# Another order for the first batch item of a fused attention and maxout-MLP kernel

One core of one Trainium2 chip. The metric is the device time of one launch in microseconds (us), the median of the runs. All other times are us from the start of the profiled span, unless marked ns.

## The reference, cut

```python
# q, k, v: [4, 8, 768, 64] fp32; sort_net: [4, 8, 8, 8]
for _ in range(5):                      # softmax rows, then normalise columns
    P = softmax_rows(P); P = P / P.sum(-2)
k_sorted = einsum('bhij,bhjcd->bhicd', P, k_blocks)     # 8 blocks of 96 rows
v_sorted = einsum('bhij,bhjcd->bhicd', P, v_blocks)
x = softmax(q_b @ k_sb.T / 8) @ v_sb    # inside each block, then heads side by side: [3072, 512]
out = maximum(x @ w1, x @ w2) @ w_out   # w1, w2: [512, 1024], w_out: [1024, 512]
```

The kernel uses max(a, b) = relu(a - b) + b: it forms W1 - W2 on VectorE (`w_difference`), h = x(W1 - W2), g = relu(h), and folds W2·W_out into one matrix, for which W2 is transposed (`w2_transposes`).

## The kernel before

These are the parts that the argument needs. The kernel gives TensorE, ScalarE (ACT) and VectorE (DVE) their instructions in program order, and in the timelines ACT and DVE run them in that order. "A" and "D" name the engine that evicts a PSUM tile.

```python
psum = tile_pool(bufs=4)                # four PSUM tiles in all
def keep_streaming(ps, n): ...          # filler: n columns of matmuls on zeros into a fresh tile

load_v(0, 0, 3); load_k(0); load_q(0)   # one queue, in this order
load_w(w2_sb, moe_w2)
load_w_columns(w1_sb, moe_w1, 0, 1); load_w_columns(w1_sb, moe_w1, 1, 2); load_w_columns(w1_sb, moe_w1, 2, 4)
...
def turn_v(rows, eng, c0, c1):          # v's (c, d) turned to (d, c)
    dst = v_dc[rows, 0 : D * BLK].rearrange("p (d c) -> p d c", c=BLK)[:, :, c0:c1]
    src = v_raw[rows].rearrange("p (c d) -> p d c", d=D)[:, :, c0:c1]
    ...                                 # nc.scalar.copy or nc.vector.tensor_copy
...
def moe_h_products(b, ch, t, hps, n=0):
    if hps[0] == 0:
        h_ps[0] = ps_f32("h_ps"); keep_streaming(h_ps[0], n)
    for m in range(2):
        for hp in hps: matmul(h_ps[0][:, m*512 : m*512+TCH], ..., start=(hp == 0), stop=(hp == 3))
...
# the first batch item
sort_k(0, 0, 3072, "A"); sort_k(0, 1, 256, "A"); sort_k(0, 2, 256, "D")
q_transposes(0, 0, "A"); sort_v(0, 0, 256, "D"); q_transposes(0, 1, "A"); sort_v(0, 1, 256, "D")
scores(0, 0, 512); sort_v(0, 2, 256, "D"); SC[1](); sort_v(0, 3, 256, "A")
...                                     # selections
SC[2](); SC[3](); VA[0](); VA[1](); values(0, 2, 1024); VA[3]()
w_difference(0); SC[4](); x_transposes(0, 0, "A"); w2_out = w2_transposes(0, "D")
x_transposes(0, 1, "A"); w_difference(1); moe_h(0, 0, 0, "A", n=1024); w2_out(); SC[5]()
# then: VA4, w_difference(2); h tile 1, SC6, SC7, VA5, w_difference(3); h tile 2, ...
```

`SC[u]` are scores u with their exp (e) on ACT, `VA[u]` values u with their normalisation on DVE.

The softmax here doesn't subtract the row's maximum and nothing guards it: scores larger than these inputs give would overflow.

## Time and profile before

| | before |
|---|---|
| median (range) of the first 3 runs | 186.23 (185.96 to 186.98) |
| span of the profiled run | 184.2 |
| granted clock over the span | 1.000 |
| first query transpose, start | 15.80 |
| g of h tile 0, start | 29.37 |
| third h product, start | 32.17 |
| fourth h product, start | 34.53 |

The last four rows are read from the timeline of TensorE and ACT. From the fourth h product on, both kernels run the same order. In rows of the timeline and of the chain of work, the first number is the start and the second the length. Groups of matmuls are named by the PSUM tile they write: tq query transposes, v_ps v sorts, s_ps scores, o_ps values, tx x transposes, tw W2 transposes, h_ps h products.

### The profile page before, as it was taken

What the parts mean: (1) busy time and instruction counts of PE and PEld (TensorE: products, weight loads), DVE (VectorE), ACT (ScalarE), POOL (GpSimd) and SP (SyncE); (2) the same over time, 40 slices, a digit from 0 to 9 for tenths busy, and PEclk for the clock granted to TensorE, in tenths of its full rate; (3) what the DMA queues carried; (4) which work ended last, traced back from release to release, by engine and by line L of the source; (5) the groups of instructions that cost most, each with busy time, mean ns of one, the idle gap of its engine ahead of it and who ended that gap; (6) DMA issues with size and microseconds to landing.
All of it is one profiled execution on the core that took longest, in us unless ns stands there. A gap on an engine that the chain in (4) does not pass through costs nothing.

```text
span 184.2 us, 4604 instructions
## 1 busy us (share of the span) xinstructions
PE 172.1 (93%) x2050; PEld 102.7 (56%) x2069; DVE 95.5 (52%) x189; ACT 93.8 (51%) x111; POOL 21.5 (12%) x38
## 2 busy tenths in 40 slices
PE   7969789999999899999999999999999999999990
PEld 2337675756564555557655555767645456654460
DVE  5887796669722655284816544355526444420030
ACT  3599866779447504355956451665463513431001
POOL 7851222200450000002000000000000000000000
PEclk9999999999999999999999999999999999999999
DMA  3999999999199972036600220200002032000241
GB/s 60 202 202 211 201 206 216 191 204 190 21 175 219 202 202 104 12 117 75 99 0 4 114 105 12 114 4 4 0 5 114 0 117 114 0 0 4 114 166 61
DMA packets 13427, 19.17 MB, mean 104 GB/s; under 512 B 800, under 2 KB 7840, under 8 KB 13408
## 3 DMA queue, kind: packets, MB, share of 16 engines
q0 software_dynamic: 9792, 12.58, 40.3%
q1 hardware_dynamic: 3328, 6.10, 8.6%
q8 instruction: 16, 0.26, 0.6%
q10 hardware_dynamic: 288, 0.20, 0.3%
q14 instruction: 3, 0.02, 0.0%
HBM read 25.17 MB, written 6.29 MB: 171 GB/s over the span
## 4 chain that ended last, share of the span: by engine, by line
PE 80%; DMA 7%; ACT 4%; DVE 3%; issue 2%; POOL 2%; ACTq 0%; POOLq 0%
PE out_ps L557 32%; PE h_ps L530 22%; DMA q_raw<-in_q_dram 6%; PE v_ps L370 4%; PE wc_ps L498 4%; PE o_ps L420 4%; PE k_ps L349 3%; PE s_ps L395 3%; PE tx_ps L452 3%; PE tq_ps L319 2%; DVE o L98 1%; ACT o L96 1%; DMA out_dram<-o 1%; PE tw_ps L475 1%; PE tq_ps L324 1%
## 5 line engine op out<-in xcount | busy, mean ns | idle before, releaser
L557 PE MATMUL out_ps<-wo_sb,g 128*128 128x512 bf16 (+1 forms) x185 | 46.0, 370 | 2.4 <-ACT o L96 0.7
L530 PE MATMUL h_ps<-xT,w_sb 128*128 128x384 bf16 x256 | 46.4, 326 | 0.3
L544 ACT ACTIVATE g<-h_ps 128x768 bf16<-128x768 f32 x27 | 21.9, 812 | 21.0 <-PE h_ps L530 21.0
L403 ACT ACTIVATE e<-s_ps 96x768 bf16<-96x768 f32 x32 | 24.3, 803 | 15.9 <-PE s_ps L395 15.9
L530 PEld LDWEIGHTS <-w_sb 128*128 128x128 bf16 x256 | 23.5, 98 | 14.9 <-issue 0.5
L557 PEld LDWEIGHTS <-g 128*128 128x128 bf16 x200 | 17.4, 98 | 16.6 <-issue 1.3
L557 PE MATMUL out_ps<-wc,xT 128*128 128x512 bf16 (+1 forms) x100 | 24.8, 370 | 0.0
L437 DVE TENSOR_TENSOR x<-o_ps,rs 96x512 bf16<-96x512 f32 x32 | 22.0, 686 | 1.1
L431 DVE RECIPROCAL rs<-o_ps 96x8 f32<-96x8 f32 x32 | 6.4, 200 | 25.5 <-PE o_ps L420 25.4
L98 DVE CAST v_sb<-v_ps 96x1024 bf16<-96x1024 f32 x9 | 11.0, 1221 | 12.2 <-PE v_ps L370 12.2
L96 ACT COPY o<-out_ps 128x1024 f32<-128x1024 f32 x6 | 6.1, 1012 | 19.6 <-PE out_ps L557 10.0
L557 PEld LDWEIGHTS <-xT 128*128 128x128 bf16 x100 | 9.8, 98 | 11.0
L98 DVE COPY o<-out_ps 128x1024 f32<-128x1024 f32 x5 | 6.1, 1225 | 16.3 <-PE out_ps L557 16.3
L188 DVE COPY v_dc<-v_raw 64x1536 bf16<-64x1536 bf16 (+2 forms) x9 | 14.0, 1591 | 0.0
L420 PEld LDWEIGHTS <-e 96*128 96x128 bf16 x256 | 11.2, 98 | 4.8 <-issue 0.6
L420 PE MATMUL o_ps<-v_sb,e 96*128 96x65 bf16 x256 | 12.7, 194 | 0.7 <-ACT v_sb L96 0.6
L370 PEld LDWEIGHTS <-v_dc 64*128 64x128 bf16 x256 | 8.1, 95 | 3.4 <-issue 2.4
L96 ACT CAST kT<-k_ps 128x1024 bf16<-128x1024 f32 x10 | 9.9, 1010 | 0.0
L78 PE MATMUL pe<-fill 128*128 128x512 bf16 x26 | 8.7, 512 | 1.2 <-DVE fill L72 1.2
L96 ACT COPY xT<-tx_ps 128x768 bf16<-128x768 bf16 x9 | 7.2, 795 | 5.1 <-PE tx_ps L452 5.1
L96 ACT CAST v_sb<-v_ps 96x1024 bf16<-96x1024 f32 x7 | 7.0, 1015 | 5.4 <-PE v_ps L370 5.4
L370 PE MATMUL v_ps<-bd,v_dc 64*128 64x64 bf16 x256 | 9.5, 190 | 0.0
(74 smaller groups left out, 164.0 us busy)
## 6 DMA issues: line engine op xcount, KB each, us to landing
out_dram<-o SPq DMA_DIRECT2D x11, 512.0 KB, 2.8
k_raw<-in_k_dram POOLq DMA_DIRECT2D x12, 256.0 KB, 13.7
q_raw<-in_q_dram POOLq DMA_DIRECT2D x4, 768.0 KB, 9.4
v_raw<-in_v_dram POOLq DMA_DIRECT2D x6, 384.0 KB, 11.9
w_sb<-in_moe_w_dram POOLq DMA_DIRECT2D x3, 512.0 KB, 15.1
wo_sb<-in_moe_w_out_dram POOLq DMA_DIRECT2D x2, 512.0 KB, 19.8
v_raw<-in_v_dram POOLq DMA_DIRECT2D x3, 256.0 KB, 5.0
w_sb<-in_moe_w_dram POOLq DMA_DIRECT2D x2, 256.0 KB, 15.7
```

The source lines that it names most:

```text
L78: nc.tensor.matmul(ps[:, 0:w], fill[:, 0:128], fill[:, 0:w], start=True, stop=True)
L96: nc.scalar.copy(out=out_ap, in_=in_ap)
L98: nc.vector.tensor_copy(out=out_ap, in_=in_ap)
L188: nc.vector.tensor_copy(out=dst, in_=src)
L370: nc.tensor.matmul(ps[:, m * 64 : (m + 1) * 64], v_dc[r0 : r0 + 64, d * BLK : d * BLK + 128], bd_v[b][r0 : r0 + 64, :], start=True, stop=True,
L403: nc.scalar.activation(out=e[:, 0 : 8 * BLK].rearrange("p (t f) -> p t f", t=2), in_=ps[0:BLK].rearrange("p (t f) -> p t f", t=2)[:, :, 0 ...
L420: nc.tensor.matmul(ps[:, h2 * 512 + ii * 65 : h2 * 512 + (ii + 1) * 65], e[:, (h2 * 4 + ii) * BLK : (h2 * 4 + ii) * BLK + 128], v_sb[:, m0 ...
L437: nc.vector.tensor_tensor(out=x, in0=ov[:, :, :, 0:D], in1=rs.to_broadcast([BLK, 2, 4, D]), op=ALU.mult,)
L498: nc.tensor.matmul(wc_ps[0][:, m * 512 : (m + 1) * 512], w2T[:, fb, dmt * 128 : (dmt + 1) * 128], wo_sb[:, fb, :], start=(fb == 0), stop=( ...
L530: nc.tensor.matmul(h_ps[0][:, m * 512 : m * 512 + TCH], w1_sb[:, hp, fb * 128 : (fb + 1) * 128], xT[:, b % 2, ch, hp % 2, hp // 2, :], sta ...
L544: nc.scalar.activation(out=g, in_=src, func=AF.Relu)
L557: nc.tensor.matmul(dst, g_tiles[b, ch, m // 2][:, m % 2, off : off + 128] if m < NFB else xT[:, b % 2, ch, hp % 2, hp // 2, off : off + 12 ...
```

## The change

Its intent: sort all of v before the second query half, so that values can follow the first scores at once; have the keys' block diagonal sooner; begin the h products of two tiles when only half of xT is there; and have the first columns of W1 and W2 early enough for that. The diff, cut:

```diff
-    load_w(w2_sb, moe_w2)
+    load_w_columns(w2_sb, moe_w2, 0, 2)
     load_w_columns(w1_sb, moe_w1, 0, 1)
     load_w_columns(w1_sb, moe_w1, 1, 2)
+    load_w_columns(w2_sb, moe_w2, 2, 4)
     load_w_columns(w1_sb, moe_w1, 2, 4)
@@ turn_v: a new argument flip; with it the copy's loops are (c, d), d innermost
+            dst = v_dc[rows, 0 : D * BLK].rearrange("p (d c) -> p c d", c=BLK)[:, c0:c1]
+            src = v_raw[rows].rearrange("p (c d) -> p c d", d=D)[:, c0:c1]
@@ block_diagonals: keys' product, reduction and result first, then those of the values
@@ moe_h_products: h_ps[t] in place of h_ps[0]
@@ the softmax steps
-            turn_v(first, "A", 0, 8)    ...  turn_v(first, "A", 8, 16)
-    turn_v(first, "A", 16, 32)
+            turn_v(first, "A", 0, 11)   ...  turn_v(first, "A", 11, 22)
+    turn_v(first, "A", 22, 32, True)
@@ the first batch item, as it is afterwards
+    sort_k(0, 0, 3072, "A"); sort_k(0, 1, 512, "A"); sort_k(0, 2, 256, "D")
+    q_transposes(0, 0, "D")
+    sort_v(0, 0, 0, "A"); sort_v(0, 1, 256, "D"); sort_v(0, 2, 256, "A"); sort_v(0, 3, 256, "D")
+    scores(0, 0, 256); SC[1]()
+    q_transposes(0, 1, "A")
+    w_difference(0)
+    values(0, 0, 1024); VA[1](); SC[2](); SC[3](); values(0, 2, 512); VA[3]()
+    x_transposes(0, 0, "A"); SC[4]()
+    moe_h_products(0, 0, 0, (0, 2), 512)
+    x_transposes(0, 1, "A"); w_difference(1)
+    moe_h_products(0, 0, 1, (0, 2))
+    moe_h(0, 0, 0, "A", (1, 3))
+    ...                                  # selections
+    SC[5](); w2_transposes(0, "D")()
@@ later: h tile 1 is finished where it was computed
+            units[1] = lambda: moe_h(0, 0, 1, "A", (1, 3))
```

More of the change, by code (lines that the diff above doesn't have):

```diff
@@ L179, with turn_v @@
     load_k(1)
-    def turn_v(rows, eng, c0, c1):
-        dst = v_dc[rows, 0 : D * BLK].rearrange("p (d c) -> p d c", c=BLK)[:, :, c0:c1]
-        src = v_raw[rows].rearrange("p (c d) -> p d c", d=D)[:, :, c0:c1]
+    def turn_v(rows, eng, c0, c1, flip=False):
+        if flip:
+            dst = v_dc[rows, 0 : D * BLK].rearrange("p (d c) -> p c d", c=BLK)[:, c0:c1]
+            src = v_raw[rows].rearrange("p (c d) -> p c d", d=D)[:, c0:c1]
+        else:
+            dst = v_dc[rows, 0 : D * BLK].rearrange("p (d c) -> p d c", c=BLK)[:, :, c0:c1]
+            src = v_raw[rows].rearrange("p (c d) -> p d c", d=D)[:, :, c0:c1]
         if eng == "A":
@@ L255, in block_diagonals @@
         keep_streaming(pe, n)
-        kinds = [1] if b % 2 else [0, 1]
+        kinds = [1] if b % 2 else [1, 0]
         for m in kinds:
@@ L269, in block_diagonals @@
             )
-        m0, nk = kinds[0], len(kinds)
-        pm = const.tile([128, 2, NB, NB], FP32, tag="pm", name="pm")
         for m in kinds:
+            pm = const.tile([128, NB, NB], FP32, tag=f"pm{m}", name="pm")
             nc.vector.tensor_tensor(
-                out=pm[:, m],
+                out=pm,
                 in0=pe[:, m * 64 : m * 64 + 64].rearrange("p (i j) -> p i j", j=NB),
@@ L278, in block_diagonals @@
             )
-        pt = const.tile([128, 2, NB], FP32, tag="pt", name="pt")
-        nc.vector.reduce_sum(out=pt[:, m0:2], in_=pm[:, m0:2], axis=AX.X)
-        bd = const.tile([128, 2, 8, NB], BF16, tag=f"bd{b}", name="bd")
-        for m in kinds:
+            pt = const.tile([128, NB], FP32, tag=f"pt{m}", name="pt")
+            nc.vector.reduce_sum(out=pt, in_=pm, axis=AX.X)
+            bd = const.tile([128, 8, NB], BF16, tag=f"bd{m}{b}", name="bd")
             nc.vector.tensor_tensor(
-                out=bd[:, m],
+                out=bd,
                 in0=maskM[:, m].to_broadcast([128, 8, NB]),
-                in1=pt[:, m].to_broadcast([128, NB, 8]).transpose([0, 2, 1]),
+                in1=pt.to_broadcast([128, NB, 8]).transpose([0, 2, 1]),
                 op=ALU.mult,
             )
-        if b % 2 == 0:
-            bd_v[b] = bd_v[b + 1] = bd[:, 0].rearrange("p m i -> p (m i)")
-        bd_k[b] = bd[:, 1].rearrange("p m i -> p (m i)")
+            if m:
+                bd_k[b] = bd.rearrange("p m i -> p (m i)")
+            else:
+                bd_v[b] = bd_v[b + 1] = bd.rearrange("p m i -> p (m i)")
     v_sb = big.tile([BLK, 128, D + 2], BF16, tag="v_sb", name="v_sb")
@@ L524, in moe_h_products @@
         if hps[0] == 0:
-            h_ps[0] = ps_f32("h_ps")
-            keep_streaming(h_ps[0], n)
+            h_ps[t] = ps_f32("h_ps")
+            keep_streaming(h_ps[t], n)
         for m in range(2):
@@ L530, in moe_h_products @@
                 nc.tensor.matmul(
-                    h_ps[0][:, m * 512 : m * 512 + TCH],
+                    h_ps[t][:, m * 512 : m * 512 + TCH],
                     w1_sb[:, hp, fb * 128 : (fb + 1) * 128],
@@ L539, in moe_h @@
         moe_h_products(b, ch, t, hps, n)
-        ps = h_ps[0]
+        ps = h_ps[t]
         g = gpool.tile([128, 2, TCH], BF16, tag="g", name="g")
@@ L616 @@
             selections(0)
-            turn_v(first, "A", 0, 8)
+            turn_v(first, "A", 0, 11)
         if it == 3:
-            turn_v(first, "A", 8, 16)
-    turn_v(first, "A", 16, 32)
+            turn_v(first, "A", 11, 22)
+    turn_v(first, "A", 22, 32, True)
     turn_v(first, "A", 32, 40)
@@ L627 @@
     sort_k(0, 0, 3072, "A")
-    sort_k(0, 1, 256, "A")
+    sort_k(0, 1, 512, "A")
     sort_k(0, 2, 256, "D")
-    q_transposes(0, 0, "A")
-    sort_v(0, 0, 256, "D")
-    q_transposes(0, 1, "A")
-    sort_v(0, 1, 256, "D")
-    scores(0, 0, 512)
-    sort_v(0, 2, 256, "D")
-    SC[1]()
-    sort_v(0, 3, 256, "A")
+    q_transposes(0, 0, "D")
+    sort_v(0, 0, 0, "A")
+    sort_v(0, 1, 256, "D")
+    sort_v(0, 2, 256, "A")
+    sort_v(0, 3, 256, "D")
+    scores(0, 0, 256)
+    SC[1]()
+    q_transposes(0, 1, "A")
+    w_difference(0)
+    values(0, 0, 1024)
+    VA[1]()
+    SC[2]()
+    SC[3]()
+    values(0, 2, 512)
+    VA[3]()
+    x_transposes(0, 0, "A")
+    SC[4]()
+    moe_h_products(0, 0, 0, (0, 2), 512)
+    x_transposes(0, 1, "A")
+    w_difference(1)
+    moe_h_products(0, 0, 1, (0, 2))
+    moe_h(0, 0, 0, "A", (1, 3))
     for b in range(1, B):
         selections(b)
-    SC[2]()
-    SC[3]()
-    VA[0]()
-    VA[1]()
-    values(0, 2, 1024)
-    VA[3]()
-    w_difference(0)
-    SC[4]()
-    x_transposes(0, 0, "A")
-    w2_out = w2_transposes(0, "D")
-    x_transposes(0, 1, "A")
-    w_difference(1)
-    moe_h(0, 0, 0, "A", n=1024)
-    w2_out()
     SC[5]()
+    w2_transposes(0, "D")()
     def turn(rows, c0):
```

## The prediction

> **What bounds the kernel now.** I read the busy slices first, then the stretches of the span, then the chain of work that ended last, then the timeline of the first 40 us for TensorE, ScalarE (ACT) and VectorE (DVE). Times are us from the span's start.
>
> The stretches (busy time of each engine in each):
>
> ```profile
> 0.00:15.80 15.80, 12.60 (x133) 5.74 (x133) 12.04 (x58) 10.38 (x13) 10.04 (x20) 1.00 0.94 162
> 15.80:37.20 21.40, 19.64 (x344) 14.41 (x346) 15.32 (x29) 16.15 (x20) 5.20 (x9) 1.00 1.20 205
> 37.20:75.00 37.80, 36.86 (x442) 21.24 (x448) 21.89 (x36) 19.28 (x22) 4.62 (x8) 1.00 0.83 160
> ```
>
> The first number after the comma is TensorE. From 37 us on it is busy 97% (36.86 of 37.80), the granted clock is 1.00 throughout, and the change touches nothing there but the list of who evicts what. So the change can act only before 37 us, and what it wins or loses there should be handed on to the end almost in full.
>
> The chain in that part (start, length, what):
>
> ```profile
> 5.07 10.68 DMA q_raw<-in_q_dram
> ...
> 15.80 0.86 PE tq_ps L324 x24
> ...
> 21.02 0.81 ACT e L403
> 21.82 0.99 ACT v_sb L96
> ...
> 22.86 0.67 PE o_ps L420 x16
> ...
> 27.35 0.81 ACT xT L96
> ...
> 28.20 1.14 PE h_ps L530 x6
> 29.33 0.28 PE s_ps L395 x8
> 29.61 0.36 PE o_ps L420 x8
> 29.97 1.32 PE h_ps L530 x8
> 31.31 0.82 ACT g L544
> ...
> 32.17 1.47 PE h_ps L530 x8
> 33.67 0.82 ACT g L544
> ...
> 34.53 1.46 PE h_ps L530 x8
> ```
>
> Two things are to be seen. Until 15.76 the end is set by the load of q, issued at 5.07; nothing ahead of it in the queue changes. After that, TensorE and the evictions take turns: e, v_sb, xT and g on ACT are links of the chain.
>
> The four PSUM tiles go round: tile n is given out when tile n-4 has been evicted. Counting the allocations from the code, the third h tile is 29 and the second is 25, and the timeline agrees: that eviction (g) ends at 31.31 + 0.81 = 32.12 and the third h product starts at 32.17. So there is some 0.05 from an eviction's end to the matmul behind it. I use this rule for the new order.
>
> **What the Trainium skill says.** (1) "PSUM — Partial Sum Buffer", the four PSUM rules: an output lies in one 2 KiB bank, and a group's first matmul clears the bits of its whole bank. The two halves of an h tile are 512 columns each, so a bank each, and a product begun on half of xT may stay open while other tiles are written. No profile of before shows this; it has no half-begun product. (2) "ScalarE: Activation LUTs", What ACT_TABLE_LOAD costs: 186 ns + 0.833 ns per element, and ACTIVATEs behind each other overlap by about 93 ns. The trace agrees for e (768 elements: 826 ns by the page, 803 measured; a pair takes 1.50, so 0.70 from start to start). It disagrees for the turning copies of v: 512 elements should be 613 ns and take 1050 to 1066, 1024 take 2046, so 1.9 ns an element or 0.12 us a column. (3) "DMA: Bandwidth & Descriptors", Issuing engines are not separate DMA queues: all transfers share 16 engines, so moving W pieces only changes their order; the trace moves about 205 GB/s all through the start. (4) "TensorE: Matmul & The Clock Gate", What's actually happening: the clock drops after an idle window of some 3.4 us. The clock stays 1.00 before, and no gap that I find below is over 1.1 us, so I charge nothing for the changed filler matmuls.
>
> **The change part by part.**
>
> *Keys' block diagonal first, turning of v.* Before, the two masks' products, one reduction and the two results run from 11.69 to 12.76 on DVE, then the first key sort starts at 12.98. With the keys' three operations alone (0.23, 0.22, 0.22, some 0.73 with gaps, as for the second item at 37.40) they are ready at 12.42, and the filler ends at 12.87: about 0.1 sooner. One more reduction makes DVE's turning copy end at about 15.4, not 15.11. ACT turns 22 columns in its idle time among the softmax steps, not 16: 6 x 0.12 = 0.7 sooner free, so its key casts start at 13.9, not 14.55. All of it lies beside the q load, which ends at 15.76. Worth 0.
>
> *W by columns.* The queue's waits let me date the landings: first half of W2 near 19.6, second 21.8, first W1 columns 23.1. Issued by columns, the first W1 columns come 0.26 MB, or 1.3 us at 205 GB/s, after the first W2 piece: about 20.9. Before, the first W difference runs at 26.66, long after its data. So this only makes the earlier place in DVE's order possible. Worth 0 itself.
>
> *New order from 15.80.* Durations: query transposes 0.79 of TensorE per half, a v sort 0.56, filler of 256 0.21, scores 0.25, values 0.27, x transposes 0.35, W2 transposes 0.87, a whole h product 1.30 and so a half 0.65; ACT v_sb 1.01, qT 1.44, e 0.81, xT 0.79, g 0.81 (0.09 less from start to start); DVE v_sb 1.22, qT 0.95, values' pair 0.83.
> - TensorE: first query half to 16.59, four v sorts with three fillers to 19.46 (16.59 + 4 x 0.56 + 3 x 0.21), filler and scores 0 and 1 to 20.20, second query half to 21.00, filler and values 0 and 1 to 21.97. Values 0 start at 21.45, against 22.86 before: a lead of 1.4.
> - ACT: v_sb to 18.28 and to 19.81, e0 20.05 to 20.86, e1 to 21.57, then qT's second half to 22.91 (1.44 behind e1). Scores 2 need it: TensorE waits from 21.97 to 22.96. This takes 1.0 of the lead.
> - Scores 2 and 3 to 23.46; e2 to 24.16, e3 to 24.87; values 2 at 24.22, values 3 at 24.92 to 25.20. Two waits on ACT, 0.8 together with the filler in them.
> - x transposes 0 to 25.56, xT 25.72 to 26.51; scores 4; half of h0 from 26.56 to 27.20; x transposes 1 to 27.55; xT 27.72 to 28.51; meanwhile half of h1; rest of h0 28.56 to 29.20; its g starts at 29.37. Before, that g starts at 29.37 too. The 1.4 are spent.
> - What is done by then: before, h0 and the first W2 transposes (0.87); after, h0 and half of h1 (0.65). After is 0.2 behind.
> - Now the PSUM tiles. After: scores 5 to 29.45; the W2 transposes take h0's tile, so they wait for g0 (30.18) until 30.24 and run to 31.10: 0.8 of waiting. Values 4 and the rest of h1 to 32.02, its g to 33.00. Scores 6 take h1's tile, so they start at 33.05: 1.0 of waiting, with nothing put beside it. Scores 6, 7 and values 5 to 33.80, third h at 33.98 (its W difference is behind the later W2 copy on DVE). Before it is at 32.17. There, scores 6, 7 and values 5 ran while g was being made, so that the round trip was filled.
> - Balance at the third h product: 33.98 - 32.17 = +1.8. Sum: 0.2 behind, + 0.8 + 1.0 waits, + 0.2 for the W difference, - 0.4 of waiting that before has at this place (31.8 to 32.17).
>
> From there both have the same order and both wait for g before the fourth h. So 186.23 + 1.8 = 188.0 by the plain sum.
>
> *Side effect.* The host-side balance of ACT against DVE starts from other totals (I worked through it: 12 of 82 later evictions change engine, among them o of the second and third item and a g). TensorE idles only 2.1 in all between 37 us and the end for evictions and the like, so I put it at plus or minus 0.5.
>
> **The rivals.**
> (A) *The lead holds.* Values start 1.4 sooner and the h products start sooner; if ACT delivers qT's second half sooner than 22.9, or h0 ends by 27.5, the end comes 1 us sooner: about 185.2. For it: the change has been laid out with care (filler sizes, exactly four tiles between the h1 halves), which smells of tuning against the chip. Against: e1 and qT on ACT in program order.
> (B) *Nothing moves*, as the load of q and then W, v and k paces the start anyway: 186.2. For it: about 205 GB/s until 45 us. Against: after 15.8 the chain of before holds no load.
> (C) *ACT's and PSUM's round trips replace the waits removed*: +1.8, 188.0, as above.
> (D) *W late*: if the first W1 columns land at 23 and not 20.9, the W difference at the head of DVE holds up the values' evictions and everything after: another +0.5 to 1, 188.8.
>
> **Range and chances.** C is what the arithmetic gives, but it sums twenty steps of which several may be off by 0.2, and A has the care of the layout for it. I weigh C and D together at 70%, B at 12% and A at 18%, and take a little off C: 187.6. Range 185.2 to 189.2. Faster by over 2% means below 182.5, which is more than all the waits before 37 us hold: 2%. Slower by over 2% means above 189.95, for which D must add itself to C: 4%. Within 2%: 94%.
>
> **What would show it.** Right: query transposes still start at 15.80; values 0 near 21.5; a wait of some 1.0 before scores 2 released by ACT's qT; g0 near 29.4; a wait of 0.8 before the W2 transposes and of 1.0 before scores 6, both released by ACT's g; the third h product near 34.0. Wrong: g0 before 28.5, or TensorE busy through 29 to 33 us; a W difference waiting for a load (then D); another start of the query transposes; or a stretch after 37 us whose length differs by over 0.5, which would be the changed evictions.

## The result, and the profile after

The changed kernel took 188.52 us (median of 4 runs, 187.97 to 188.58), the kernel before 186.09 (185.95 to 186.98). The ratio is 1.0114, with a 95% interval of 1.0076 to 1.0151. Here and below a ratio is the mean time of one kernel's fast runs over that of the other's in the same rounds, so not quite the ratio of the medians. The verdict is: slower by 1.1%, which is within 2%.

The busy slices of the changed kernel have a line that the kernel before does not have (its line holds nines alone):

```profile
PEclk9999699999999999999999999999999999999999
```

The stretches of the changed kernel (TensorE, weight loads, DVE, ACT, GpSimd, then granted clock, DMA share and GB/s), to be laid beside those in the prediction:

```profile
15.80:37.20 21.40, 18.96 (x313) 13.40 (x314) 14.20 (x27) 15.05 (x19) 5.18 (x9) 0.92 1.22 205
37.20:75.00 37.80, 37.19 (x460) 21.85 (x459) 22.26 (x38) 20.41 (x24) 4.62 (x8) 1.00 0.79 147
```

In the first stretch the mean clock is 0.92 and TensorE issues 313 matmuls where it issued 344. After 37 us nothing got worse. In finer stretches (TensorE alone) the changed kernel shows where the clock went:

```profile
18.00:20.00 2.00, 1.92 (x47) 1.00 1.43 192
20.00:22.00 2.00, 1.97 (x34) 0.54 1.28 206
22.00:24.00 2.00, 2.00 (x31) 0.60 1.26 213
24.00:26.00 2.00, 1.54 (x32) 1.00 1.22 200
```

For 3.4 us from 20.2 on, TensorE ran at half clock. The chain of work through the changed part:

```profile
15.68 1.82 ACT kT L96 x2
17.50 0.04 issue
17.54 0.27 PE v_ps L78
...
20.54 0.76 PE s_ps L399 x16
21.30 1.44 PE tq_ps L328 x23
...
22.76 1.45 ACT qT L96
...
24.25 0.36 PE s_ps L399 x8
...
30.70 0.28 PE s_ps L399 x8
30.97 1.01 PE tw_ps L479 x16
...
32.01 1.22 DVE w2T L98
...
33.41 0.57 issue
33.99 0.69 DVE w_sb L514
...
34.72 1.49 PE h_ps L534 x8
```

Three things differ from the prediction. The second v sort waits for ACT's key casts, which end at 17.50. The second query transposes take 1.44 at half clock, not 0.79. And the third h product waits for a W difference on DVE. What the prediction had right is the wait of scores 2 (24.25) for ACT's qT, right behind it.

The W2 transposes start at 30.97, while this eviction of h tile 0 (timeline of the changed kernel) is still running, until 31.54:

```profile
30.73 0.81 ACT L548 ACTIVATE g<-h_ps 128x768 bf16<-128x768 f32 x1 [0.90 <-PE h_ps L534]
```

So they did not wait for that tile. Scores 6 did not wait for h tile 1 either: they start in the timeline before its eviction (32.92 to 33.73) does.

```profile
32.81 0.82 PE L399 MATMUL s_ps<-qT,kT 64*128 64x96 bf16 x16
```

| from the timelines | before | after | difference |
|---|---|---|---|
| first query transpose to start of g0 ("head") | 13.57 | 14.91 | +1.34 |
| start of g0 to third h product ("tail") | 2.80 | 3.99 | +1.19 |
| third to fourth h product | 2.36 | 2.37 | 0.01 |
| fourth h product to end of span | 149.7 | 149.7 | 0 |

The spans differ by 2.6 (186.8 against 184.2), and all of it arises between 15.8 and 34.7. The twelve later evictions that change engine cost nothing that shows.

### The profile page after: what moved, and what is told of

It is laid out like the page before. It is cut to its first block, busy times and chain, and to the rows that moved or that the text cites. A ratio compares the mean times of both kernels' runs of the same rounds, so it can differ in the third digit from the quotient of the medians.

```text
span 186.8 us, 4622 instructions
## 1 busy us (share of the span) xinstructions
PE 175.1 (94%) x2068; PEld 103.6 (55%) x2068; DVE 95.7 (51%) x191; ACT 95.1 (51%) x111; POOL 22.9 (12%) x38
## 4 chain that ended last, share of the span: by engine, by line
PE 79%; ACT 8%; DVE 8%; DMA 2%; issue 1%; ACTq 0%
PE out_ps L561 32%; PE h_ps L534 22%; PE v_ps L374 4%; PE wc_ps L502 4%; ACT v_dc L191 3%; PE o_ps L424 3%; PE s_ps L399 3%; PE k_ps L353 3%; PE tx_ps L456 3%; PE tq_ps L323 2%; DVE o L98 1%; DMA out_dram<-o 1%; PE tw_ps L479 1%; ACT kT L96 1%; ACT e L407 1%
## 5 line engine op out<-in xcount | busy, mean ns | idle before, releaser
L561 PE MATMUL out_ps<-wo_sb,g 128*128 128x512 bf16 (+1 forms) x200 | 48.1, 371 | 1.4 <-DVE o L98 0.6
L548 ACT ACTIVATE g<-h_ps 128x768 bf16<-128x768 f32 x26 | 21.1, 812 | 21.4 <-PE h_ps L534 21.4
L98 DVE COPY o<-out_ps 128x1024 f32<-128x1024 f32 x6 | 7.3, 1224 | 17.8 <-PE out_ps L561 17.8
L98 DVE CAST v_sb<-v_ps 96x1024 bf16<-96x1024 f32 x7 | 8.5, 1220 | 12.0 <-PE v_ps L374 12.0
L96 ACT COPY o<-out_ps 128x1024 f32<-128x1024 f32 x5 | 5.1, 1012 | 17.6 <-PE out_ps L561 17.6
L550 DVE TENSOR_SCALAR g<-h_ps 128x768 bf16<-128x768 f32 x6 | 5.7, 957 | 12.3 <-PE h_ps L534 12.3
L96 ACT CAST v_sb<-v_ps 96x1024 bf16<-96x1024 f32 x9 | 8.9, 1014 | 5.8 <-PE v_ps L374 5.8
L122 POOL DMA_DIRECT2D q_raw<-in_q_dram x4 | 5.7, 1433 | 46.9 <-DVE q_pair L308 44.5
L96 ACT COPY xT<-tx_ps 128x768 bf16<-128x768 bf16 x10 | 8.0, 796 | 5.2 <-PE tx_ps L456 5.2
## 6 DMA issues: line engine op xcount, KB each, us to landing
w_sb<-in_moe_w_dram POOLq DMA_DIRECT2D x3, 512.0 KB, 15.8
```

The lines of the kernel that those rows point to most:

```text
L96: nc.scalar.copy(out=out_ap, in_=in_ap)
L98: nc.vector.tensor_copy(out=out_ap, in_=in_ap)
L548: nc.scalar.activation(out=g, in_=src, func=AF.Relu)
L561: nc.tensor.matmul(dst, g_tiles[b, ch, m // 2][:, m % 2, off : off + 128] if m < NFB else xT[:, b % 2, ch, hp % 2, hp // 2, off : off + 12 ...
```

## The experiments

Each call ran on one chip beside the kernel before. Most of these profiles differ from those of the first chip in a way that matters: the clock was also at half for 3.4 us between 11 and 16, where TensorE waits for the softmax and then for q. This moves the start of the query transposes to 16.6 to 17.0 (15.5 to 16.4 in the profiles without it). The kernel before has a span of 183.9 to 184.2 in its runs at 0.999 or 1.000 and of 185.2 to 186.0 in those at 0.990 or 0.991. That scatter is as large as the effect. So I read the head and the tail of each profile, both of which begin after it, and give the ratio beside them.

It is not the chip that parts these profiles: b2_new_head, b3_hidden and c3_filler_256 lost no early stretch on chips where others did. In the clock records of the 14 packed traces, every stretch at full or at half clock (but for the last one of a trace) lasts a whole number of 3.41 us, so the changes fall on a grid. The first full-clock stretch starts at 4.1 to 5.8 in the nine profiles with the early loss and at 6.2 to 7.2 in the five without. So where the grid lies against the program goes with that loss; why it lies there in a run is not shown.

| run | ratio to before (95%) | head | tail | clock in the head |
|---|---|---|---|---|
| before (first chip) | 1 | 13.57 | 2.80 | 1.00 |
| the change (first chip) | 1.0114 (1.0076 to 1.0151) | 14.91 | 3.99 | 3.4 us at half |
| a1_noflip | 1.0119 (1.0058 to 1.0180) | 15.20 | 3.98 | 3.4 us at half |
| a2_fill | 1.0101 (1.0041 to 1.0161) | 14.77 | 3.99 | 1.00 |
| a3_oldtail | 1.0055 (1.0002 to 1.0109) | 14.90 | 2.80 | 3.4 us at half |
| a4_oldtail_noflip | 1.0055 (1.0000 to 1.0109) | 15.01 | 2.80 | 3.4 us at half |
| b1_q_dve | 1.0034 (0.9975 to 1.0093) | 13.21 | 3.99 | 1.00 |
| b2_new_head | 0.9952 (0.9905 to 1.0000) | 13.32 | 2.80 | 1.00 |
| b3_hidden | 1.0021 (0.9975 to 1.0068) | 13.82 | 2.80 | 1.00 |
| b4_no_filler | 1.0020 (0.9933 to 1.0107) | 16.09 | 2.80 | half for most of it |
| c1_difference_first | 1.0113 (1.0055 to 1.0171) | 15.15 | 3.38 | 3.4 us at half |
| c2_less_filler | 1.0055 (1.0000 to 1.0110) | 15.39 | 2.80 | 3.4 us at half |
| c3_filler_256 | 0.9996 (0.9940 to 1.0051) | 13.36 | 2.79 | 1.00 |
| d1_change_again | 1.0145 (1.0093 to 1.0196) | 15.09 | 3.99 | 3.4 us at half |

The tail is the cleanest number here: 2.79 to 2.80 wherever the old order stands from scores 4 on, 3.98 to 3.99 with the new one, whatever the clock did earlier.

**a1_noflip: the flipped copy.**

```diff
-    turn_v(first, "A", 22, 32, True)
+    turn_v(first, "A", 22, 32)
```

> The changed kernel, but ACT turns v's columns 22 to 32 in the same order of elements as all the others (not with the inner loop across the stride). Theory F (that flipped copy is what is slow): the five ACT copies end near 13.8 instead of 15.7, the key casts start at about 13.9 instead of 15.59, and the second v sort no longer waits for a key cast (17.54 becomes about 17.37). On the clock two ways: if the gap of 0.28 us at 17.3 is what lowered it, the granted clock is 1.000 and the time falls by about 1.5 to 187.0; if the four v sorts in a row keep TensorE too lightly loaded whatever the gap, the clock stays at 0.991 and the time is 188.2 to 188.4.

The groups by form of the changed kernel show the price of the flip:

```profile
L191 ACT COPY v_dc<-v_raw 64x640 bf16<-64x640 bf16 x1 | 3.4, 3371 | 0.0
```

and of this run:

```profile
L191 ACT COPY v_dc<-v_raw 64x640 bf16<-64x640 bf16 x1 | 1.3, 1262 | 0.0
```

The same 640 elements take 3.37 us with the output's stride innermost and 1.26 in the other order. Without the flip the five copies end at 13.96, as expected, and the v sorts follow each other every 0.79 us without a wait; in the changed kernel the first two are 1.11 apart. So the flip cost 0.3 on the first chip. On this chip the query transposes started 1.2 later, which hides it, and the time did not improve. The key casts did not start at 13.9 either: they waited until 15.32 for key sorts that ran at half clock here. The clock fell all the same (21.8 to 25.3), this time behind a pause of 0.84 that TensorE makes anyway (last section). So the flip is not needed for the fall; whether a gap is, this run does not tell.

**a2_fill: 512 columns of filler before each v sort.**

```diff
-    sort_v(0, 0, 0, "A"); sort_v(0, 1, 256, "D"); sort_v(0, 2, 256, "A"); sort_v(0, 3, 256, "D")
+    sort_v(0, 0, 512, "A"); sort_v(0, 1, 512, "D"); sort_v(0, 2, 512, "A"); sort_v(0, 3, 512, "D")
```

> The changed kernel with the flipped copy kept and 512 columns of filler before each of the four v sorts (0, 256, 256, 256 in the change). Theory K (the clock's fall to half from 20.2 to 23.6 us is caused by too little TensorE activity between 15.8 and 20.2): the granted clock is 1.000; the four fillers cost about 0.2 + 3 x 0.1 = 0.5 us of TensorE, the half clock cost 1.5 to 1.7 us of TensorE time of which some lies beside ACT; net 187.4 to 188.0. Rival: the fall has to do with the run's phase or is caused by something other than activity: clock 0.991 and 188.9 to 189.0.

The clock stayed at 1.00 from 16 us on in the profiled run, and in two of the four runs (0.995 and 1.000) hardly any was lost. The time did not fall: what the clock gave back, the filler took (query transposes to values 0: 6.70, against 5.98 in b1_q_dve, which has the thin filler and no clock loss there; so 0.72). This profile shows the wait on ACT's qT free of any clock loss, in its timeline:

```profile
25.10 0.52 PE L399 MATMUL s_ps<-qT,kT 64*128 64x96 bf16 x16 [0.90 <-ACT qT L96]
```

**a3_oldtail and a4_oldtail_noflip: the old order from scores 4 on.**

```diff
-    x_transposes(0, 0, "A"); SC[4](); moe_h_products(0, 0, 0, (0, 2), 512); x_transposes(0, 1, "A")
-    w_difference(1); moe_h_products(0, 0, 1, (0, 2)); moe_h(0, 0, 0, "A", (1, 3)); ...; SC[5](); w2_transposes(0, "D")()
+    SC[4](); x_transposes(0, 0, "A"); w2_out = w2_transposes(0, "D"); x_transposes(0, 1, "A")
+    w_difference(1); moe_h(0, 0, 0, "A", n=1024); w2_out(); ...; SC[5]()
-            units[1] = lambda: moe_h(0, 0, 1, "A", (1, 3))
```

> The changed kernel with everything from scores 4 to scores 5 put back as before: W2 transposes between the two x transposes, h tile 0 whole, h tile 1 whole in its old place. Theory C of the prediction (the waits of W2 transposes on g0 and of scores 6 on g1, two of 0.8 to 1.0 us, are the price of the half-begun products): faster than the changed kernel by about 1.5, 187.0. Rival (the loss comes from the sort order, the clock and the flipped copy alone): within 0.4 of the changed kernel, 188.1 to 188.9.

> As the one before, and with the copy not flipped. If flip and tail are independent: the gain of both adds up, 186.8 if the clock still falls and 185.5 if it does not. If it is at or above 186.1 with the clock at 1.000, the new sort order has itself nothing to give.

The tail falls from 3.99 to 2.80, 1.2 where 1.5 was expected, and the ratio from 1.012 or 1.010 to 1.0055 in the same rounds. So the half-begun products, with the W2 transposes behind them, cost 1.2. Not flipping adds nothing on this chip, for the reason above. The heads of 14.90 and 15.01 come with a clock loss.

**b1_q_dve: the second query half evicted by DVE.**

```diff
-    q_transposes(0, 1, "A")
+    q_transposes(0, 1, "D")
```

> The changed kernel with the second query half evicted by DVE, not ACT (one letter). Theory Q (scores 2 wait for that eviction behind both e's on ACT): DVE is free, so the eviction starts as soon as its transposes end and takes 0.95 instead of 1.44; scores 2 start 0.5 sooner where the clock is at half there, 0.9 sooner where it is not, and the whole is 0.5 to 0.9 faster than the changed kernel, 187.7 on a chip with the first one's timing (ratio to before 1.006 to 1.009). Rival (the g waits further on swallow it): ratio 1.011 as the change.

Its chain of work, where the clock was at 1.00:

```profile
21.42 0.79 PE tq_ps L328 x24
...
22.59 0.69 PE o_ps L424 x16
23.28 0.35 PE s_ps L399 x8
```

From the end of the transposes (22.21) to scores 2 it is 1.07. In a2_fill, also at full clock, it is 25.10 - 23.13 = 1.97, so the step is worth 0.9. In the changed kernel it is 24.25 - 22.74 = 1.51: at half clock the e's had got further by then, and the step is worth 0.44. Both as expected; the ratio (1.0034, forecast 1.006 to 1.009) came out better, and in the profiled run the head kept its clock. This run also gives the size of the clock loss. From the first score to the end of the query transposes it needs 22.21 - 20.91 = 1.30; the changed kernel needs 22.74 - 20.48 = 2.26. The half clock cost TensorE 0.96 here, and scores 2 about 0.5, as the step's 0.9 shrank to 0.44.

**b2_new_head, c2_less_filler, c3_filler_256: the new sort order on its own.** All three have the old order from scores 4 on, no flip, qT's second half on DVE, and the first W difference after values 3. They differ in the filler before the four v sorts: 512 each, then 0, 256, 256, 256, then 256 each.

```diff
@@ b2_new_head, against a4_oldtail_noflip
-    sort_v(0, 0, 0, "A"); sort_v(0, 1, 256, "D"); sort_v(0, 2, 256, "A"); sort_v(0, 3, 256, "D")
+    sort_v(0, 0, 512, "A"); sort_v(0, 1, 512, "D"); sort_v(0, 2, 512, "A"); sort_v(0, 3, 512, "D")
-    q_transposes(0, 1, "A"); w_difference(0)
+    q_transposes(0, 1, "D")
     ...; VA[3]()
+    w_difference(0)
```

> The new sort order alone, freed of what the runs so far blame: copy not flipped, 512 columns of filler before each v sort, second query half on DVE, first W difference after values 3, and from scores 4 on the old order. From the start of the query transposes to the fourth h product it should take 20.1 (as measured with the old tail) less 1.4 (clock) less 0.9 (query half) = 17.8, against 18.7 of before: 0.9 faster than before, ratio 0.995. Rival: the new order only exchanges one wait for another: 18.7 or more, ratio 1.000 to 1.005.

> The new sort order as in the earlier run that had 512 columns before each v sort, with the change's own filler (0, 256, 256, 256). With the clock at 1.00 the stretch from the first query transpose to the fourth h product is 18.48 - 0.7 = 17.8, spans near 183.3; if the thinner filler lets the clock fall in that stretch in some runs, those lose 0.8 and more and the median is no better than before, ratio 0.995 to 1.002.

> As the one before with 256 columns before the first v sort too. Between the two: stretch 18.0 with the clock at 1.00, ratio to before 0.992 to 0.998. If the clock is decided by filler between 0 and 512 columns, this one has fewer runs below 0.99 than the one before.

At full clock the head is 13.32 and 13.36, against 13.57 of before: ahead by 0.2, not by the 0.9 expected. From first query transpose to fourth h product b2_new_head took 18.48 where 17.8 was forecast: I had taken the clock for 1.4, which b1_q_dve puts at 0.96, and the eviction by DVE for 0.9, which is 0.44 beside half clock. (The thicker filler, 0.72, and the pause of the last section, 0.61 in a3_oldtail and none here, were not in the forecast; with them the sum is 18.8, so 0.3 stays unexplained.) c3_filler_256 took 18.51 where 18.0 was forecast: its thinner filler saves 0.1 for each v sort, and the pause (0.29) takes most of that back. At a clock of 1.000 the spans are 183.7 to 184.0 (b2) and 183.4 to 183.6 (c3), against 183.9 to 184.1 of before. No version beats the kernel before clearly. The ratio of b2_new_head came out as forecast (0.995) by luck: the stretch was 0.7 longer than forecast, and six of the seven runs of the kernel before beside it had lost clock. Those of c2_less_filler (1.0055) and c3_filler_256 (0.9996) are above their forecasts.

Less clock is lost with more filler. Runs with a granted clock of 0.985 or more: 4 of 4 with 512 each, 5 of 6 with 256 each, 2 of 6 with the change's own filler, and 18 of 18 of the kernel before beside them. The counts are small and from two chips.

**b3_hidden: the parts put at 0, in the kernel before.** W by columns, keys' block diagonal first, ACT turning 11, 11 and 10 columns in place of 8, 8 and 16 (not flipped).

```diff
-    load_w(w2_sb, moe_w2)
+    load_w_columns(w2_sb, moe_w2, 0, 2)
...
+    load_w_columns(w2_sb, moe_w2, 2, 4)
@@ block_diagonals as in the change
-    turn_v(first, "A", 16, 32)
+    turn_v(first, "A", 22, 32)
```

> The kernel before with only those parts of the change that the prediction put at 0: W1 and W2 by columns in the new order of loads, keys' block diagonal first, ACT turning 11, 11, 10 (not flipped) columns where it turned 8, 8, 16. Expected ratio 0.998 to 1.002 and the query transposes start within 0.2 of what they do in the other runs of this chip. Rival D of the prediction (the columns delay something): ratio 1.004 or more and a wait on a W load in the profile.

The ratio's interval, 0.9975 to 1.0068, holds 1. The tail is that of before and no wait on a W load shows. The query transposes start at 15.54, not within 0.2 of the chip's other runs as forecast (16.4 to 16.8), which goes with the early loss of clock in two of the three; the head is longer by 0.25, which is the pause described last (0.58 against 0.33). So these parts move nothing, and rival D of the prediction is out.

**b4_no_filler: the kernel before without its filler in this part.**

```diff
-    sort_v(0, 0, 256, "D"); ...; scores(0, 0, 512); ...; values(0, 2, 1024)
+    sort_v(0, 0, 0, "D"); ...; scores(0, 0, 0); ...; values(0, 2, 0)
```

> The kernel before without the filler matmuls ahead of its four v sorts, scores 0 and values 2 (2560 columns, some 1.5 us of TensorE). If the filler is what keeps the clock in this stretch, the granted clock falls to half somewhere between 19 and 27 us as in the changed kernel and the time is 0.5 to 1.5 worse than before, 187 to 188. If filler does nothing for the clock, the clock is as before and the time is the same or up to 0.5 better.

Finer stretches of TensorE in its profiled run:

```profile
20.00:22.00 2.00, 0.65 (x20) 0.89 1.38 193
22.00:24.00 2.00, 1.93 (x43) 0.50 1.35 204
...
28.00:30.00 2.00, 2.00 (x24) 0.50 1.24 207
```

The clock fell near 21.5 and stayed at half for 10 us. Three of its four runs are at 0.973 or below. The one run at 1.000 has a span of 183.6, 0.3 below the kernel before at that clock. Of the kernel before, 1 run of 7 beside it was at 1.000 and none below 0.985. So in this stretch the filler buys clock and, by that one run, costs 0.3. The fall in this profile comes behind a pause of 1.58 (last section), so filler and pause are not separated.

**c1_difference_first: what the third h product waits for.**

```diff
-    SC[5](); w2_transposes(0, "D")()
+    SC[5](); w2_out = w2_transposes(0, "D"); w_difference(2); w2_out()
-        0: [VA[4], lambda: w_difference(2)],
+        0: [VA[4]],
```

> The changed kernel with the third W difference moved ahead of the W2 eviction in DVE's order (DVE is idle from 29 to 32 there). In the changed kernel's profile the third h product waits for that difference (33.99 to 34.67), not for a PSUM tile. Theory W: it then starts right behind values 5, about 0.6 sooner, and the stretch from the start of g0 to the start of the third h product goes from 3.99 to about 3.4; whole time about 0.6 better than the change, ratio 1.008 where the change has 1.011. Rival, the rule of the prediction (tile n waits for the eviction of tile n-4, so W2 transposes for g0 and scores 6 for g1): the stretch stays within 0.2 of 3.99.

Timeline of this run:

```profile
29.85 0.67 DVE L514 TENSOR_TENSOR w_sb<-w_sb 128x1024 bf16<-128x1024 bf16 x1
...
31.80 0.81 ACT L548 ACTIVATE g<-h_ps 128x768 bf16<-128x768 f32 x1 [0.90 <-PE h_ps L534]
...
33.88 0.82 PE L399 MATMUL s_ps<-qT,kT 64*128 64x96 bf16 x16
...
35.18 1.46 PE L534 MATMUL h_ps<-xT,w_sb 128*128 128x384 bf16 x8
```

35.18 - 31.80 = 3.38, exactly the expected 3.4. So half of the tail's 1.19 was the W difference waiting in DVE's order behind the W2 eviction, and the rule of the prediction, as it was used there, is refuted. The ratio, 1.0113, does not show the 0.6: two of the four runs lost two stretches of clock (0.982) and a third nearly as much (0.985).

The starts also take the other half apart. From the start of g0 to scores 6 it is 1.84 before (29.37 to 31.21), 2.08 in the changed kernel and 2.08 here: 0.24, as the W2 transposes now lie in this stretch and only half of h tile 1 does. From scores 6 to the third h product it is 0.96 before, 1.91 in the changed kernel and 1.30 here: 0.34 more than before, and 0.61 for the W difference. In the 1.30 lie two short waits: scores 7 start 0.04 after the W2 eviction ends (34.31) and values 5 start 0.05 after the second g ends (34.79); in the changed kernel it is 0.06 (33.23) and 0.05 (33.73).

**d1_change_again: the change itself, for a run without clock loss.**

> The change itself once more, to catch runs of it in which the clock never falls: of its four runs so far each had lost clock (0.991 or 0.996), while the kernel before has many at 1.000 with a span of 183.9. Theory (the order costs 1.7, the lost clock 0.8 to 1 on top): a run at 1.000 has a span of 185.4 to 185.8, one at 0.991 186.5 to 187.2, one at 0.982 187.5 to 188.2. Rival (the clock is all of it, the order costs nothing): a run at 1.000 has a span of 183.8 to 184.3.

No run came out at 1.000. The best is at 0.995 with a span of 186.2; beside it, the kernel before has 184.0 and 184.2 at 0.999. Half a window of lost clock lies between, so at most 0.9 of these 2.1 is clock and at least 1.2 is order. The others are at 0.989 (187.5), 0.979 to 0.982 (187.9 to 188.9) and 0.971 (188.8). The runs at 0.982 are up to 0.7 longer than expected.

## Why the prediction was right or wrong, point by point

The sum gave 188.0, of which 187.6 was made as the forecast; measured were 188.52, inside the range of 185.2 to 189.2. The place, the sign and the hand-over to the end were right. Two errors of opposite sign lie inside the sum: g0 came 1.36 later than forecast, and the stretch from it to the third h product was 3.99 where the forecast had 4.61. So it was partly luck that the number came this near.

- **The query load sets the start, and nothing ahead of it changes: right.** The transposes start at 15.82, against 15.80. W by columns and the block diagonal are worth 0: right (b3_hidden).
- **ACT free 0.7 sooner: wrong.** The flipped copy was costed like the others at 0.12 us a column. It took 3.37 in place of 1.2, and ACT's key casts began at 15.59, not 13.9. Cost on the path: 0.3, on the first chip only.
- **Nothing charged for the clock: wrong.** The prediction said that no gap is over 1.1 us and so charged nothing. The clock fell with no such gap: in the 3.41 us before the fall TensorE was idle for 0.39 in all, 0.28 of it the wait for the key casts and 0.11 the pause of the last section. It cost TensorE 0.96 in the profiled run, and some clock was lost in all ten runs of the change. Fewer runs lost it with more filler (b2_new_head, c3_filler_256), so the loss goes with what TensorE does in this stretch.
- **The wait of scores 2 for ACT's qT: right.** 1.0 was said (without a clock loss), 0.90 measured at full clock (a2_fill), and taking it away gave that back (b1_q_dve).
- **g0 at 29.37, a tie: wrong by 1.36.** The forecast has scores 0 at 19.67 (19.46 and 0.21 of filler), the end of the query transposes at 21.00 and scores 2 at 22.96; the changed kernel has 20.48, 22.74 and 24.25, so it is 0.81, 1.74 and 1.29 late. Of the 0.81, 0.3 is the flip; most of the rest is TensorE's own work and pause, costed too low (b1_q_dve, at full clock and without that wait, takes 4.30 up to scores 0, where the forecast has 3.87). The half clock then adds 0.9, and some 0.45 of it does no harm, as ACT's qT no longer waits behind the e's.
- **Two PSUM waits of 0.8 and 1.0 in the tail: the size was too large and the cause wrong.** The step that failed is "the four PSUM tiles go round: tile n is given out when tile n-4 has been evicted". It held for the kernel before, where every tile is finished in the order in which it was begun. With two h tiles held open, the W2 transposes did not take h tile 0's memory: they ran while it was being evicted; and scores 6 did not wait for h tile 1's. It would fit that a new tile takes the memory that came free earliest; this I infer from three starts in the trace (the W2 transposes at 30.97, scores 7 at 33.29, values 5 at 33.78) and did not test by itself. The tail's cost was 1.19, not 1.8 (0.2 behind, 0.8 and 1.0 of waits, 0.2 for the W difference, less 0.4). By c1_difference_first it is 0.24 of work left over (0.2 in the prediction), 0.34 with two short waits for other tiles (1.4 in the prediction, 1.8 less the 0.4) and 0.61 for the W difference behind the W2 eviction on DVE (0.2). All of it goes away with the old order (a3_oldtail).
- **Changed evictions later, plus or minus 0.5: right, 0.** The part after the fourth h product is equal to 0.1.
- **The rivals.** A (the lead holds) fails: values 0 start at 23.48 in the changed kernel, later than the 22.86 of before. B and D fail too. C stands in its main claim, that round trips through ACT and PSUM eat the lead; its second round trip goes through DVE.

What stays open is what tips the clock. It is not the busy share of TensorE alone. Below, TensorE in the 3.41 us before the fall in the changed kernel, then in a stretch of the same grid in a2_fill, which no fall follows:

```profile
16.77:20.18 3.41, 3.02 (x68) 1.00 1.39 197
```

```profile
22.01:25.42 3.41, 2.51 (x74) 1.00 1.25 209
```

Nor is it the pause alone. In the seven profiles of the later chips that lost clock in the head, the pause was 0.6 to 1.6; in those that kept it, it was 0.3 or less, but for b3_hidden with 0.58. But the changed kernel on the first chip lost it with a pause of 0.11, and the kernel before kept it there with 0.33. More filler makes TensorE reach the pause later and shortens it, so no run parts thin filler and pause further. Why runs of one kernel on one chip differ is open too, but for the place of the 3.41 us grid named above.

## What to carry to other kernels

Before moving work forward, follow the engine that must evict it in its own program order: here ACT's eviction of qT behind two e's (at full clock), and a W difference behind a W2 copy on DVE, each took back part of what the new order won. When a chain of small matmuls replaces a mix of small and large ones, look at the granted clock in 1 to 2 us stretches and over several runs, as the mean over the span hides it. And in short stretches compare from event to event inside the trace, not whole times, where lost clock scatters the latter by up to 2 us.

## What the Trainium skill lacked or had wrong

- "TensorE: Matmul & The Clock Gate", What's actually happening, has the clock at half after at least one idle window. Here it fell to half after a stretch with work in it: of the 3.41 us before 20.18 TensorE was busy for 3.02. A later section of that page (A second HAM failure mode: psum-queue depth-cycling) does say that short idle times between groups of matmuls can make the clock swing, but not how much is too much; here 2.51 of 3.41 was followed by no fall (a2_fill). That the fall lasts about 3.4 us, or a multiple of it (some 10 us in b4_no_filler), agrees with the page.
- "ScalarE: Activation LUTs", What ACT_TABLE_LOAD costs, gives 0.833 ns an element and says nothing on access order. "Advanced Engine Details and Errata", SBUF Cachelines, has a penalty where each access is to another cacheline, but no figure for it on ScalarE. A bf16 copy with the source's inner step at 64 elements took about 1.9 ns an element (1024 elements in 2.0 us); with the destination's inner step at 96 elements and the source contiguous, 3371 ns for 640, some 5 ns an element.
- "Runtime: NRT & Kernel Launch", Instruction fetch mechanics, calls the cost of crossing from one block of instructions to the next mostly hidden. Here TensorE pauses after its 223rd weight load, wherever in the program that falls, with nothing that it waits for in the profile. Below, the kernel before and b4_no_filler, each up to the pause (x is the count of matmuls, then of weight loads), and the row after it. The pause was 0.1 to 1.6 us in 13 of the 14 profiles, b2_new_head being without one. It would fit a fetch of instructions behind the loads: in the packed traces the first packet of 16384 bytes on the instruction queue ends 1.3 to 1.6 us before the weight loads go on in all 13, and 2.2 before in b2_new_head. No run tests it. The prediction had no term for it.

```profile
0.00:19.80 19.80, 16.42 (x223) 8.66 (x223) 14.81 (x60) 13.99 (x16) 10.57 (x21) 1.00 0.98 172
...
19.95 0.28 PE L78 MATMUL v_ps<-fill 128*128 128x256 bf16 x1 [0.33 <-issue]
```

```profile
0.00:20.50 20.50, 15.71 (x222) 8.54 (x223) 15.08 (x60) 13.94 (x16) 11.11 (x22) 0.92 0.99 170
...
21.35 0.66 PE L370 MATMUL v_ps<-bd,v_dc 64*128 64x64 bf16 x12 [1.58 <-issue]
```
